# Attention values of the lead tiles: three bursts of two steps, every normalisation one step behind its sums

## The chip, the cores and the metric

One core of a Trainium2 chip. The metric is device time in microseconds (us) from launch to end. A profile of one execution tells which engine did what when: TensorE (PE, matmuls; PEld its weight loads), VectorE (DVE), ScalarE (ACT), GpSimd (POOL), and the DMA queues.

## The reference

```python
def _attn_ref(q, kv, w_sr):            # q (4, 12288, 128), kv (4, 384, 32, 128)
    kv_pool = kv.reshape(B, H // 4, 4, W // 4, 4, C).mean(axis=(2, 4))
    k = v = kv_pool.reshape(B, -1, C) @ w_sr        # 768 keys for each image
    s = (1 / sqrt(C)) * (q @ k.transpose(0, 2, 1))
    a = exp(s - s.max(-1, keepdims=True))
    a /= a.sum(-1, keepdims=True) + 1e-09
    return a @ v

def _moe_ref(x, w_gate, w_val, w_out):  # x = attention output, 49152 x 128; d_ff 1536
    return (maximum(x @ w_gate, 0) * (x @ w_val)) @ w_out
```

## The kernel before

Work goes in tiles of 512 queries, 96 of them. For one tile: six score matmuls (128 keys each) with an exponential (`scores`), the product with the values in two halves of two query blocks (`values`), the division by the sums (`keep_sums`, `keep_values`), a transposing DMA (`x_turn`), then twelve blocks of the feed-forward layer: value projection with a cast on ScalarE, gate projection with a product on VectorE, output projection. The sums of the exponentials come out of the same matmul as a 129th column, so sums and values share a PSUM bank:

```python
    def values(k, jc, half):                 # two matmuls of 128x129 into one bank
        ...
    def keep_sums(k, half):
        rinvs[k, half] = work.tile([128, 2, 1], FP32, tag="rinv", bufs=4, name="rinv")
        nc.vector.reciprocal(rinvs[k, half], x_banks[k, half][:, :, C : C + 1])

    def keep_values(k, half, engine=nc.vector):
        x_ps, rinv = x_banks.pop((k, half)), rinvs.pop((k, half))
        if engine is nc.scalar:
            for i in range(2):
                nc.scalar.mul(x16s[k][:, 2 * half + i, :], x_ps[:, i, 0:C], rinv[:, i])
        else:
            nc.vector.tensor_tensor(...)     # one product with the broadcast reciprocals

    def value_proj(k, fb):
        ...                                  # matmul, L236
        nc.scalar.copy(val, va_ps)           # the cast, L240
    def gate_proj(k, fb):
        ...                                  # matmul, L247; needs a bank
        nc.vector.scalar_tensor_tensor(      # the gate product, L250; needs the cast
            hTs[k][:, fb, :], g_ps, 0.0, vals.pop((k, fb)), op0=ALU.max, op1=ALU.mult)
```

The stages are software-pipelined: stage k does the scores of tile k, the values of tile k - 1, the projections of tile k - 3 and the output of tile k - 4. Stage k = 3 (LAG) is the first that has projections. In it the values that tiles 2 and 3 still lack are worked off from a list, two chunks of keys in each step. I call it the **lead stage**.

```python
    left = [(2, jc, 0) for jc in range(NJC - 2, NJC)]
    left += [(k, jc, half) for k, half in ((3, 0), (2, 1), (3, 1)) for jc in range(NJC)]
    ...
        for step in range(NFB):              # 12 steps in a stage
            ...                              # output projections
            if kF < NT:
                value_proj(kF, step)
            if k == LAG:
                own, left = left[:2], left[2:]
                for kV, jc, half in own:
                    values(kV, jc, half)
                    if jc == NJC - 1:
                        keep_sums(kV, half)                # VectorE
                        keep_values(kV, half, nc.scalar)   # ScalarE, at once
                        if half == 1:
                            x_turn(kV)
            ...
            if kF < NT:
                gate_proj(kF, step)
```

The softmax here doesn't subtract the row's maximum and nothing guards it: scores larger than these inputs give would overflow.

Of the kernel before, what the change touches and what calls it, by code (L numbers as in the profile page):

```python
# [16 lines left out]
def kernel(  # L17
# [22 lines left out]
    nc = tc.nc  # L40
# [5 lines left out]
    NJC = J // 128  # L46
# [20 lines left out]
    def bank(shape, dtype=FP32):  # L67
        return psum.tile(shape, dtype, tag="bank", name="bank_ps")
# [4 lines left out]
    def q_load(g):  # L73
        if not 0 <= g < NG:
            return
        b, n0 = divmod(g * GRP * T, N)
        q16 = work.tile([128, GRP * NS, C], FP16, tag="q16", bufs=2)
        nc.gpsimd.dma_start(  # L78
            q16, q[b, n0 : n0 + GRP * T, :].rearrange("(p s) c -> p s c", p=128)
        )  # L80
        q16s[g] = q16

    def q_turn(g):
        if not 0 <= g < NG:
            return
        q16 = q16s.pop(g)
        qT = work.tile([128, GRP * NS, 128], FP16, tag="qT", bufs=3)
        nc.sync.dma_start_transpose(qT, q16.rearrange("p s c -> p (s c)"))
        qTs[g] = qT
# [58 lines left out]
    def turn_open(b, pair):  # L148
        kv_Ts[b, pair] = bank([128, 2, 128])
# [33 lines left out]
    def scores(k, jc):  # L183
        if jc == 0:
            aTs[k] = work.tile([128, NJC, T], FP16, tag="aT", bufs=4, name="aT")
        s_ps = bank([128, T])
        nc.tensor.matmul(s_ps, kv16[:, k // NST, jc, 0:C], qT_of(k), start=True, stop=True)  # L187
        nc.scalar.activation(aTs[k][:, jc, :], s_ps, AF.Exp, scale=qk_scale)  # L188

    def values(k, jc, half):  # L190
        if jc == 0:
            x_banks[k, half] = bank([128, 2, C + 1])
            if half == 0:
                x16s[k] = work.tile([128, NS, C], FP16, tag="x16", bufs=3, name="x16")
        x_ps = x_banks[k, half]
        for i in range(2):
            s = 2 * half + i
            nc.tensor.matmul(  # L198
                x_ps[:, i, :], aTs[k][:, jc, s * 128 : (s + 1) * 128],
                kv16[:, k // NST, jc, C : 2 * C + 1],  # L200
                start=(jc == 0 and i == 0), stop=(jc == NJC - 1), skip_group_check=True,
# [12 lines that stand above are left out]
            nc.vector.tensor_tensor(  # L214
                x16s[k][:, 2 * half : 2 * half + 2, :], x_ps[:, :, 0:C],
                rinv.to_broadcast([128, 2, C]), op=ALU.mult,
            )

    def x_turn(k):
        x16 = x16s.pop(k)  # L220
        xT = work.tile([128, NS, 128], FP16, tag="xT", bufs=5, name="xT")
        nc.sync.dma_start_transpose(xT, x16.rearrange("p s c -> p (s c)"))
        xTs[k] = xT.rearrange("c s p -> c (s p)")
# [10 lines left out]
    def value_proj(k, fb):  # L234
        va_ps = bank([128, T])
        nc.tensor.matmul(  # L236
            va_ps, wv16[:, fb * 128 : (fb + 1) * 128], xTs[k], start=True, stop=True
        )
        val = work.tile([128, T], FP16, tag="val", bufs=6, name="val")
        nc.scalar.copy(val, va_ps)  # L240
        vals[k, fb] = val

    def gate_proj(k, fb):
        if fb == 0:
            hTs[k] = work.tile([128, NFB, T], FP16, tag="hT", bufs=3, name="hT")
        g_ps = bank([128, T])
        nc.tensor.matmul(  # L247
            g_ps, wg16[:, fb * 128 : (fb + 1) * 128], xTs[k], start=True, stop=True
        )
        nc.vector.scalar_tensor_tensor(  # L250
            hTs[k][:, fb, :], g_ps, 0.0, vals.pop((k, fb)), op0=ALU.max, op1=ALU.mult
        )
        if fb == NFB - 1:
            xTs.pop(k)
# [7 lines left out]
    def out_proj(k, fb):  # L262
        if fb == 0:
            o_banks[k] = bank([128, NS, 128])
        for s in range(NS):
            out_add(k, fb, s, o_banks[k][:, s, :], fb == 0 and s == 0)

    def out_scale(k, engine, own, o_ps=None):
        if k not in o_sbs:
            o_sbs[k] = work.tile([128, NS, 128], FP32, tag="o_sb", bufs=3, name="o_sb")  # L270
        o_sb, o_ps = o_sbs[k][:, own], o_ps if o_ps is not None else o_banks[k]
        if engine is nc.scalar:
            nc.scalar.mul(o_sb, o_ps, 1.0 / X_SCALE**2)
        else:
            nc.vector.tensor_scalar(o_sb, o_ps, 1.0 / X_SCALE**2, None, op0=ALU.mult)  # L275

    def out_store(k, own):
        nc.sync.dma_start(
            out[k // GRP * GRP * T : (k // GRP + 1) * GRP * T, :].rearrange(
                "(p i s) c -> i p s c", p=128, i=GRP  # L280
            )[k % GRP][:, own], o_sbs[k][:, own],
        )
        if own.stop == NS:
            for tiles in (hTs, o_banks, o_sbs):
                del tiles[k]
# [134 lines left out]
        keep_values(1, half)  # L420
    for jc in range(NJC - 2):
        values(2, jc, 0)
    left = [(2, jc, 0) for jc in range(NJC - 2, NJC)]
    left += [(k, jc, half) for k, half in ((3, 0), (2, 1), (3, 1)) for jc in range(NJC)]


    last = NT + LAG - 1
    for k in range(LAG, last + 1):
        g, ph = divmod(k, GRP)
        if ph == 1:  # L430
            q_turn(g + 1)
            q_load(g + 2)
        b = k // NST + 1
        at = k % NST - (NST - NJC - 6)
        for step in range(NFB):
            kO, kF = k - LAG - 1, k - LAG
            half, i = divmod(step // 2, NJC // 2)
            if k == LAG and step >= NFB - 4:
                out_proj(kF, step - NFB + 4)
            if k == LAG + 1 and step % 3 > 0:  # L440
                out_proj(kO, 4 + step - 1 - step // 3)
            if 0 <= kO:
                if kO > 0:
                    out_proj(kO, step)
                if step == NFB - 1 and k < last:
                    out_scale(kO, nc.vector if kF < NT - 2 else nc.scalar, slice(0, NS))
                    out_store(kO, slice(0, NS))
            if kF < NT:
                value_proj(kF, step)
            if k == LAG:  # L450
                own, left = left[:2], left[2:]
                for kV, jc, half in own:
                    values(kV, jc, half)
                    if jc == NJC - 1:
                        keep_sums(kV, half)
                        keep_values(kV, half, nc.scalar)
                        if half == 1:
                            x_turn(kV)
            elif step % 2 == 0:
                if k < NT:  # L460
                    scores(k, step // 2)
            elif k > GRP and k - 1 < NT:
                values(k - 1, 2 * i, half)
                values(k - 1, 2 * i + 1, half)
                if i == NJC // 2 - 1:
                    keep_sums(k - 1, half)
                    keep_values(k - 1, half)
                    if half == 1:
                        x_turn(k - 1)
            if kF < NT:  # L470
                gate_proj(kF, step)
            if k == LAG and step == 2:
                x_turn_pe(1)
            if b < B:
                if step == 1 and 0 <= at < NJC and at % 2 == 0:
                    kv_load(b, at // 2)
                if step == 3 and 0 <= at - 2 < NJC:
                    pool_pixels(nc.gpsimd, b, (at - 2) // 2, at % 2)
                pair = (at - 5) // 2
                if at % 2 == 1 and 0 <= pair < NJC // 2:  # L480
                    if step == 2:
                        turn_open(b, pair)
                        turn_add(b, pair, s3s.pop((b, pair))[:, :, None], True, True)
                    if step == 4:
                        project(b, pair)
                    if step == 8:
                        turn_values(b, pair)
# [33 lines left out]
```

## Time and profile before

| of the kernel before | value | where from |
|---|---|---|
| time | 1048.1 us (three runs, 1048.07 to 1048.92) | timed runs |
| TensorE in the chain that ended last | 97% | page |
| steady step, four matmul slots | 0.876 us | starts of the value projections |
| lead stage, k = 4, k = 5 | 8.95, 9.36, 10.67 us | order of time, starts of the value projections |
| ScalarE idle for the reciprocal (L212 for L206) | 1.5 us, three times | the waits |

The prediction shows the lines on which this rests. The first 32 us of the kernel (loads, first scores) belong to no part of the change.

### The profile page before, as it was taken

The page shows a single profiled execution, that of the slowest core. Times are in us where ns is not written, and L with a number is a line of the kernel's source. Part 1 is how long each engine was busy: PE and PEld are TensorE (multiplying, and loading weights), DVE is VectorE, ACT ScalarE, POOL GpSimd, SP SyncE. Part 2 cuts the span into 40 slices and gives each one's busy share as a digit, 9 for nine tenths or more (in the row PEclk, how much of TensorE's full clock was granted, in tenths as well). Part 3 has the DMA queues.
Part 4 walks back from the last instruction along what each step waited for, and adds up shares of the span by engine and source line. Part 5 has one row for each costly group of instructions (what it writes and reads, how often), then busy time and mean ns, then how long its engine had stood idle before and what let it go on. Part 6 is the DMA issues. An engine that isn't in the chain of part 4 may idle for free.

```text
span 1045.5 us, 25976 instructions
## 1 busy us (share of the span) xinstructions
PE 1036.0 (99%) x9984; PEld 690.1 (66%) x9984; DVE 913.3 (87%) x1679; ACT 908.9 (87%) x1741; POOL 107.8 (10%) x127
## 2 busy tenths in 40 slices
PE   8999999999999999999999999999999999999998
PEld 6566666666666666666666666666666666666665
DVE  3798889898988888998888888889988888888898
ACT  3888888888888888888888888888888888888887
POOL 2000045200000015500000003440000000000000
PEclk9999999999999999999999999999999999999999
DMA  8733256241422335623224134551331322212111
GB/s 302 120 82 74 79 177 167 52 87 32 87 53 65 72 125 138 157 57 72 58 60 87 31 87 132 150 150 41 77 65 53 72 65 54 67 32 67 32 47 47
DMA packets 125853, 90.75 MB, mean 87 GB/s; under 512 B 103328, under 2 KB 104224, under 8 KB 125728
## 3 DMA queue, kind: packets, MB, share of 16 engines
q1 hardware_dynamic: 120144, 75.78, 26.8%
q0 software_dynamic: 5440, 13.24, 7.7%
q8 instruction: 78, 1.28, 0.5%
q14 instruction: 47, 0.39, 0.1%
q10 hardware_dynamic: 144, 0.07, 0.0%
HBM read 52.76 MB, written 25.17 MB: 75 GB/s over the span
## 4 chain that ended last, share of the span: by engine, by line
PE 97%; DMA 1%; SPq 1%; DVE 0%; ACT 0%; issue 0%; DVEq 0%
PE bank_ps L257 25%; PE bank_ps L247 24%; PE bank_ps L236 24%; PE bank_ps L198 12%; PE bank_ps L187 12%; DMA parts<-in_kv_dram 1%; PE bank_ps L156 1%; PE bank_ps L168 1%; SPq L128 0%; ACT aT L188 0%; SPq L93 0%; PE bank_ps L176 0%; DVE kv L169 0%; DVE kvT L163 0%; PE bank_ps L229 0%
## 5 line engine op out<-in xcount | busy, mean ns | idle before, releaser
L250 DVE SCALAR_TENSOR_TENSOR hT<-bank_ps,val 128x512 f16<-128x512 f32 x1152 | 759.5, 687 | 100.9 <-ACT val L240 74.7
L240 ACT CAST val<-bank_ps 128x512 f16<-128x512 f32 x1152 | 677.7, 591 | 111.8 <-PE bank_ps L236 107.5
L257 PEld LDWEIGHTS <-hT 128*128 128x128 f16 x4608 | 351.4, 98 | 200.1 <-issue 0.9
L257 PE MATMUL bank_ps<-wo,hT 128*128 128x128 f16 x4608 | 443.1, 219 | 0.0
L236 PE MATMUL bank_ps<-xT,wv 128*128 128x512 f16 x1152 | 436.6, 379 | 0.0
L247 PE MATMUL bank_ps<-xT,wg 128*128 128x512 f16 x1152 | 435.7, 378 | 0.0
L188 ACT ACTIVATE aT<-bank_ps 128x512 f16<-128x512 f32 x576 | 346.0, 604 | 16.9 <-PE bank_ps L187 16.6
L198 PE MATMUL bank_ps<-kv,aT 128*128 128x129 f16 x2304 | 223.3, 219 | 0.0
L198 PEld LDWEIGHTS <-aT 128*128 128x128 f16 x2304 | 177.2, 98 | 68.1 <-issue 0.6
L187 PE MATMUL bank_ps<-qT,kv 128*128 128x512 f16 x576 | 216.4, 379 | 1.1 <-DVE kv L169 0.5
L247 PEld LDWEIGHTS <-wg 128*128 128x128 f16 x1152 | 111.5, 97 | 65.8 <-issue 0.5
L236 PEld LDWEIGHTS <-wv 128*128 128x128 f16 x1152 | 112.7, 98 | 0.5
L214 DVE TENSOR_TENSOR x<-bank_ps,rinv 128x256 f16<-128x256 f32 x188 | 79.7, 424 | 6.7 <-DVE rinv L206 0.2
L78 POOL DMA_DIRECT2D q<-in_q_dram x23 | 12.5, 545 | 570.6 <-DMA qT<-q 570.4
L275 DVE TENSOR_SCALAR o_sb<-bank_ps 128x512 f32<-128x512 f32 (+1 forms) x95 | 64.0, 674 | 1.3 <-PE bank_ps L257 1.3
L139 POOL TENSOR_TENSOR s<-parts 128x512 f32<-128x512 f32 x36 | 45.3, 1269 | 162.7 <-DMA parts<-in_kv_dram 153.5
L187 PEld LDWEIGHTS <-kv 128*128 128x128 f16 x576 | 55.8, 98 | 2.4 <-DVE kv L169 1.4
L206 DVE RECIPROCAL rinv<-bank_ps 128x2 f32<-128x2 f32 x192 | 30.6, 160 | 1.6 <-PE bank_ps L198 1.6
L141 POOL TENSOR_TENSOR s<-s 128x512 f32<-128x512 f32 x18 | 22.9, 1269 | 1.4
L143 POOL TENSOR_TENSOR c<-s 128x256 f32<-128x256 f32 x18 | 13.1, 726 | 1.4
L163 DVE COPY kvT<-bank_ps 128x256 f32<-128x256 f32 x12 | 5.0, 417 | 4.5 <-PE bank_ps L156 4.5
L146 POOL TENSOR_TENSOR kv_s<-c 128x128 f32<-128x128 f32 x18 | 8.2, 456 | 1.4
(37 smaller groups left out, 81.0 us busy)
## 6 DMA issues: line engine op xcount, KB each, us to landing
parts<-in_kv_dram SPq DMA_DIRECT2D x48, 512.0 KB, 6.4
out_dram<-o_sb SPq DMA_DIRECT2D x95, 256.0 KB, 2.1
q<-in_q_dram POOLq DMA_DIRECT2D x23, 512.0 KB, 5.1
xT<-x SPq DMA_TRANSPOSE x94, 2.5
q<-in_q_dram SPq DMA_DIRECT2D x1, 768.0 KB, 8.3
wv<-in_moe_w_val_dram POOLq DMA_DIRECT2D x2, 192.0 KB, 4.3
wg<-in_moe_w_gate_dram POOLq DMA_DIRECT2D x2, 192.0 KB, 4.9
wo<-in_moe_w_out_dram POOLq DMA_DIRECT2D x1, 384.0 KB, 9.3
```

The source lines that it names most:

```text
L139: eng.tensor_tensor(s2[:, i], parts[:, 2 * i, h], parts[:, 2 * i + 1, h], op=ALU.add)
L187: nc.tensor.matmul(s_ps, kv16[:, k // NST, jc, 0:C], qT_of(k), start=True, stop=True)
L188: nc.scalar.activation(aTs[k][:, jc, :], s_ps, AF.Exp, scale=qk_scale)
L198: nc.tensor.matmul(x_ps[:, i, :], aTs[k][:, jc, s * 128 : (s + 1) * 128], kv16[:, k // NST, jc, C : 2 * C + 1], start=(jc == 0 and i == 0) ...
L206: nc.vector.reciprocal(rinvs[k, half], x_banks[k, half][:, :, C : C + 1])
L214: nc.vector.tensor_tensor(x16s[k][:, 2 * half : 2 * half + 2, :], x_ps[:, :, 0:C], rinv.to_broadcast([128, 2, C]), op=ALU.mult,)
L236: nc.tensor.matmul(va_ps, wv16[:, fb * 128 : (fb + 1) * 128], xTs[k], start=True, stop=True)
L240: nc.scalar.copy(val, va_ps)
L247: nc.tensor.matmul(g_ps, wg16[:, fb * 128 : (fb + 1) * 128], xTs[k], start=True, stop=True)
L250: nc.vector.scalar_tensor_tensor(hTs[k][:, fb, :], g_ps, 0.0, vals.pop((k, fb)), op0=ALU.max, op1=ALU.mult)
L257: nc.tensor.matmul(o_ps, hTs[k][:, fb, s * 128 : (s + 1) * 128], wo16[:, fb, :], start=first, stop=(fb == NFB - 1), skip_group_check=True,)
L275: nc.vector.tensor_scalar(o_sb, o_ps, 1.0 / X_SCALE**2, None, op0=ALU.mult)
```

## The change

Its intent: the normalisation on ScalarE shall not stand at the head of the queue before its reciprocal is there. It is issued a step later, behind the next cast. And the value matmuls, evenly two chunks a step, are gathered into bursts: three chunks in each of two steps, then a step with none, in which the two scalings lie. (The first pair of scalings is the exception: step 0 keeps its two chunks, and the scalings of its sums lie in step 1, the first step of a burst.)

```diff
-    left = [(2, jc, 0) for jc in range(NJC - 2, NJC)]
-    left += [(k, jc, half) for k, half in ((3, 0), (2, 1), (3, 1)) for jc in range(NJC)]
+    left = {0: (2, 0, range(NJC - 2, NJC))}
+    for step, k, half in ((1, 3, 0), (4, 2, 1), (7, 3, 1)):
+        left[step] = (k, half, range(NJC // 2))
+        left[step + 1] = (k, half, range(NJC // 2, NJC))
+    ready = {}
@@ in the step loop
             if k == LAG:
-                own, left = left[:2], left[2:]
-                for kV, jc, half in own:
-                    values(kV, jc, half)
-                    if jc == NJC - 1:
-                        keep_sums(kV, half)
-                        keep_values(kV, half, nc.scalar)
-                        if half == 1:
-                            x_turn(kV)
+                if step in ready:
+                    keep_values(*ready[step], nc.scalar)
+                    if ready[step][1] == 1:
+                        x_turn(ready[step][0])
+                if step in left:
+                    kV, hV, own = left[step]
+                    for jc in own:
+                        values(kV, jc, hV)
+                    if own.stop == NJC:
+                        keep_sums(kV, hV)
+                        ready[step + 1] = (kV, hV)
```

## The prediction

> **What bounds the kernel now.** I read the page's busy row first. TensorE (PE) is at 99%, but that row says little: a 128x512 matmul is listed with 379 ns, while the order of time shows the next one starting 0.22 us later. So I went to the chain of work that ended last, to see which engine holds the end.
>
> ```profile
> PE 1036.0 (99%) x9984; PEld 690.1 (66%) x9984; DVE 913.3 (87%) x1679; ACT 908.9 (87%) x1741; POOL 107.8 (10%) x127
> ...
> PE 97%; DMA 1%; SPq 1%; DVE 0%; ACT 0%; issue 0%; DVEq 0%
> ```
>
> TensorE holds 97% of the end. A change that moves work among other engines can win only where TensorE waits. The diff touches one stage, the lead stage (k = LAG = 3), the first that runs the feed-forward projections, so I put the timeline of one engine at a time over it. Its twelve steps begin with the value projections (L236) at 31.91 us and end at 40.86, where the next stage (k = 4) begins; k = 5 begins at 50.22 and k = 6 at 60.89.
>
> How much does TensorE lose there? Count slots. A slot is one 512-column matmul or four 128-column ones. A steady step has four (value projection, scores or attention values, gate projection, output projection). Between 900.22 and 942.29 the value projection starts 48 times, so a step is 42.07 / 48 = 0.876 us and a slot 0.219 us. The lead stage has 24 projections, 10 slots of attention values (20 steps of two matmuls, from the list `left`), 4 of output projection and 1 turn: 39 slots, 8.54 us; it took 8.95, a loss of 0.41. Stage k = 4 has 24 + 6 scores + 8 output slots = 38, 8.32 us; it took 9.36, a loss of 1.04. Stage k = 5 has 48, 10.51 us; it took 10.67, a loss of 0.16. Afterwards the steps are regular. **The most that any repair of the lead stage can give is 0.41 + 1.04 + 0.16 = 1.6 us, 0.15% of the time.**
>
> Why does TensorE lose it? The scalar engine's own order of time:
>
> ```profile
> 32.82 0.63 ACT L212 ACTIVATE x<-bank_ps,rinv 128x128 f16<-128x128 f32 x2
> 33.34 1.77 ACT L240 CAST val<-bank_ps 128x512 f16<-128x512 f32 x3
> 35.69 0.63 ACT L212 ACTIVATE x<-bank_ps,rinv 128x128 f16<-128x128 f32 x2 [0.57 <-DVE rinv L206]
> 36.20 1.56 ACT L240 CAST val<-bank_ps 128x512 f16<-128x512 f32 x3
> 38.22 0.63 ACT L212 ACTIVATE x<-bank_ps,rinv 128x128 f16<-128x128 f32 x2 [0.46 <-DVE rinv L206]
> 38.74 1.56 ACT L240 CAST val<-bank_ps 128x512 f16<-128x512 f32 x3
> 40.76 0.63 ACT L212 ACTIVATE x<-bank_ps,rinv 128x128 f16<-128x128 f32 x2 [0.46 <-DVE rinv L206]
> 41.27 1.56 ACT L240 CAST val<-bank_ps 128x512 f16<-128x512 f32 x3
> 42.69 0.64 ACT L188 ACTIVATE aT<-bank_ps 128x512 f16<-128x512 f32 x1
> ```
>
> At three of the four normalisations (L212) the scalar engine stands for 0.57 + 0.46 + 0.46 = 1.49 us until the reciprocal of the sums (L206) is there. The vector engine shows why that is late:
>
> ```profile
> 36.82 1.29 DVE L250 SCALAR_TENSOR_TENSOR hT<-bank_ps,val 128x512 f16<-128x512 f32 x2 [0.58 <-ACT val L240]
> 38.02 0.16 DVE L206 RECIPROCAL rinv<-bank_ps 128x2 f32<-128x2 f32 x1
> 38.10 0.67 DVE L250 SCALAR_TENSOR_TENSOR hT<-bank_ps,val 128x512 f16<-128x512 f32 x1
> ```
>
> The reciprocal stands behind the gate product (L250) of the step before, which needed a cast (L240) that ended only just before. Meanwhile the scalar engine, its queue headed by the normalisation, makes no further cast, and VectorE then idles 0.58 us for one. The two take turns: 35.69, 38.22, 40.76 is one round per three steps in 2.53 us, while TensorE's nine slots take 1.97. So TensorE runs into banks that were not emptied, and the chain in order of time says so twice:
>
> ```profile
> 38.49 0.37 ACT x L212
> 38.86 0.04 issue
> 38.90 0.38 PE bank_ps L236
> ...
> 41.04 0.35 ACT x L212
> 41.39 0.04 issue
> 41.43 0.38 PE bank_ps L187
> ```
>
> Both times the matmul wants the bank that the normalisation reads.
>
> **What the Trainium skill says.** "Trainium Kernel Development and Optimization", Performance Expectations, warns that matmul busy time is a bad metric because matmuls are pipelined; the trace agrees (379 ns listed, 0.22 us apart). "TensorE: Matmul & The Clock Gate", Part 1, gives start to start as N / 2.4 GHz plus some 2.5 ns, 216 ns for 512 columns; the trace has 0.22. "PSUM — Partial Sum Buffer", Engine vs sequencer instructions, calls the ScalarE and VectorE queues strict FIFO: the idle pieces above are that, a cast that is ready stands behind a normalisation that is not. "ScalarE: Activation LUTs", What ACT_TABLE_LOAD costs, has an ACTIVATE with a pointer operand at 280 ns + 0.833 ns an element, 387 ns for 128, with some 93 ns of overlap; the trace lists 364 ns, and a pair until the next cast takes 41.27 - 40.76 = 0.51 us.
>
> **The change, part by part.** *Removed and added work: none.* The same 40 value matmuls, four reciprocals, eight scalings and two transposing DMAs run; only positions change.
>
> *One step behind.* The queue of ScalarE now has cast, cast, scalings instead of cast, scalings, cast. The cast of the next step (0.47 us back to back: 41.27 to 42.69 is three) fills the time in which the gate product and the reciprocal run. The wait of 0.46 is removed by 0.47 of cast, the one of 0.57 all but 0.1. Saved on ScalarE: about 1.4 of 1.49 us.
>
> *Bursts.* In place of one slot of values in each of steps 0 to 9, there is one in step 0 and 1.5 in steps 1, 2, 4, 5, 7, 8, none in 3, 6, 9. Three steps still have nine slots (1.97 us); inside them the value projections are 0.77, 0.77 and 0.44 us apart instead of 0.66. The light step is the one that holds the two scalings. ScalarE needs 3 x 0.47 + 0.51 = 1.92 us for three steps, VectorE 3 x 0.61 + 0.08 = 1.91 (0.61 is half of the 1.29 of two products without their end; 0.08 from 38.02 to 38.10): all three engines come out nearly level. A cast may now wait for a matmul in a burst. Laying the casts out step by step (0.42 us from a projection's start to its cast, as 31.91 to 32.33) I find such waits of about 0.3 near the turn in step 2 and 0.45 near step 9, where output projection begins.
>
> *Sum at the start of k = 4.* Before, the cast of its first step began at 41.27 + 2 x 0.47 = 42.2; its matmul had begun at 40.86, so it was 42.2 - 41.28 = 0.9 late. After, TensorE without loss arrives at 31.91 + 8.54 = 40.45, so the cast could begin at 40.87; ScalarE gets there at 32.33 + 12 x 0.47 + 4 x 0.51 = 40.0 plus the waits of 0.8 or so and a few small ones, 40.9 to 41.1: 0.2 late at most. The two bank waits go, since each normalisation comes 1 us earlier against the same taker.
>
> *Stage k = 4.* Here ScalarE is the slower engine: its round of an exponential and two casts takes 1.43 us for two steps (42.69, 44.12, 45.56 are the exponentials), 8.58 for the stage, TensorE 8.32. Lateness grows from 0.2 to about 0.5. At 50.34, where the old kernel had recovered to 0.5 late, TensorE lost nearly nothing more; so I charge 0 to 0.3 us, plus about 0.1 for the uneven start. From k = 5 on TensorE is slower (1.75 us for two steps) and the lateness dissolves. Gain: 1.6 - 0.3 = **1.3 us**, or 1048.1 - 1.3 = **1046.8 us**.
>
> **Rivals.** (1) *The bursts starve ScalarE:* the wait for the reciprocal becomes a wait for projections. For it: the engines are level within 3%, with no slack in a round. Against: the wait sits where ScalarE would otherwise be ahead. It would halve the gain, 1047.5. (2) *VectorE becomes the bound:* its lead stage is 12 x 0.61 + 0.5 for reciprocals and the turn, near 8 us of TensorE's 8.54; it idled 0.58 a round only because of ScalarE. Gain 0.8 to 1, 1047.2. (3) *A late normalisation delays the transposing DMA, hence k = 5 and 6:* the old one was issued at 38.87 and was done in 4.05 us, k = 5 begins at 50.22, 7 us later. I expect nothing. (4) *Nothing arrives at the end:* no wait for memory stands after the stage in the chain, so what TensorE gains early it keeps.
>
> **Range and chances.** The ceiling is 1.6 us; three runs of the kernel before lie 0.85 us apart, as large as the gain. I take 1046.0 (whole ceiling and a good draw) to 1048.3 (no gain). Two per cent is 21 us, thirteen times the ceiling, so within 2% is nearly certain.
>
> **What would show it.** Right: no idle of 0.4 us or more for L206 before L212; no piece of L212 in the chain that ended last; k = 4 starting some 0.4 us and k = 5 about 1.2 to 1.5 us earlier; steady steps at 0.876 us as before. Wrong: ScalarE's idle reappearing before L240 with the value projection as releaser, or a projection held by a bank that a normalisation still owns. A shift outside 30 to 61 us would mean that something I have not seen moved.

## The result, and the profile after

| | before | after | ratio, 95% interval |
|---|---|---|---|
| first comparison, 6 runs each | 1048.43 us | 1046.67 us | 0.9988, 0.9974 to 1.0002 |
| second, 9 and 5 runs | 1047.91 us | 1046.66 us | 0.9984, 0.9972 to 0.9997 |
| third, 9 and 5 runs | 1047.82 us | 1046.58 us | 0.9991, 0.9979 to 1.0004 |

Times are medians. A ratio is the mean time of the one kernel's runs over that of the other's in the same rounds, so it is not quite the ratio of the medians. The timed runs alone barely resolve the gain: one interval of three leaves 1 out. Both kernels have the odd run at a granted clock of 0.996 or 0.997 (after: 1048.92 and 1049.16; before: 1049.67 and 1049.97), longer than the change is worth. One such execution was traced (vector_norm_timed, 0.998): all that it has more lies before the lead stage, which begins at 34.16 us against 32.57 in the other trace of that kernel. So the runs below are judged by a finer measure: **the stretch** from the first value projection of the lead stage to the first of stage k = 6, read from the order of time. All that the change can do lies in it, and it repeats: 28.98 and 28.99 us in two traces of the kernel before, 27.83, 27.83 and 27.82 in three of the kernel after. What comes behind the stretch (the span less the end of the stretch) lasts 984.6 us to within 0.1 in every trace of every run, so what is won in the stretch arrives at the end.

| us | lead stage | k = 4 | k = 5 | stretch |
|---|---|---|---|---|
| before | 8.95 | 9.36 | 10.67 | 28.98 |
| after | 8.57 | 8.63 | 10.63 | 27.83 |
| slots of 0.219 us | 39: 8.54 | 39: 8.54 | 48: 10.51 | 126: 27.6 |

The stretch is 1.15 us shorter, which agrees with medians 1.2 to 1.8 us apart. Here is ScalarE's order of time after, in the columns start, length, instruction, and idle time before it with its releaser:

```profile
32.91 1.24 ACT L240 CAST val<-bank_ps 128x512 f16<-128x512 f32 x2 [0.25 <-PE bank_ps L236]
34.05 0.63 ACT L212 ACTIVATE x<-bank_ps,rinv 128x128 f16<-128x128 f32 x2
34.56 0.59 ACT L240 CAST val<-bank_ps 128x512 f16<-128x512 f32 x1
35.34 0.58 ACT L240 CAST val<-bank_ps 128x512 f16<-128x512 f32 x1 [0.18 <-PE bank_ps L236]
35.82 0.63 ACT L212 ACTIVATE x<-bank_ps,rinv 128x128 f16<-128x128 f32 x2
36.33 1.63 ACT L240 CAST val<-bank_ps 128x512 f16<-128x512 f32 x3
37.85 0.63 ACT L212 ACTIVATE x<-bank_ps,rinv 128x128 f16<-128x128 f32 x2
38.36 1.08 ACT L240 CAST val<-bank_ps 128x512 f16<-128x512 f32 x2
39.73 0.59 ACT L240 CAST val<-bank_ps 128x512 f16<-128x512 f32 x1 [0.29 <-PE bank_ps L236]
40.21 0.63 ACT L212 ACTIVATE x<-bank_ps,rinv 128x128 f16<-128x128 f32 x2
40.73 1.57 ACT L240 CAST val<-bank_ps 128x512 f16<-128x512 f32 x3
42.14 0.65 ACT L188 ACTIVATE aT<-bank_ps 128x512 f16<-128x512 f32 x1
```

No normalisation (L212) has idle time before it. What idle time is left names the value projection (L236) as releaser: ScalarE waits for TensorE now, as it should where TensorE is the bound. VectorE, in the same stretch, stands less: before, it stood 0.58 us for a cast three times, each one product after a reciprocal; now only 0.22 us behind the reciprocal at 34.80 and 0.23 at 41.35. Around the middle one it has no idle time:

```profile
36.13 1.52 DVE L250 SCALAR_TENSOR_TENSOR hT<-bank_ps,val 128x512 f16<-128x512 f32 x2
37.56 0.16 DVE L206 RECIPROCAL rinv<-bank_ps 128x2 f32<-128x2 f32 x1
37.64 2.04 DVE L250 SCALAR_TENSOR_TENSOR hT<-bank_ps,val 128x512 f16<-128x512 f32 x3
```

And in the chain that ended last, at the place where the score matmul (L187) of k = 4 waited for a normalisation, there is now only TensorE, a slot at a time:

```profile
41.00 0.22 PE bank_ps L247
41.22 0.22 PE bank_ps L236
41.44 0.22 PE bank_ps L187
```

The span of the first trace after, 1044.9 us, is only 0.6 below the 1045.5 of before, less than the stretch gives. The rest went in the head: the lead stage began at 32.49 us against 31.91. I do not put that down to the change, which edits no instruction there. The start strays from trace to trace of one kernel (32.08 to 32.49 in three traces after; 31.79 and 31.91 in two before; 32.57 and 34.16 in two of vector_norm below, which has no bursts; 31.83 in vector_burst, which has them), and in the chain of the head it is the first loads that land later: their piece in the chain lasted 11.22 us in place of 10.82.

### The profile page after: what moved, and what is told of

Same layout as the page of the kernel before. It is cut to its first block, busy times and chain, and to the rows that moved or that the text cites. A ratio compares the mean times of both kernels' runs of the same rounds, so it can differ in the third digit from the quotient of the medians.

```text
span 1044.9 us, 25975 instructions
## 1 busy us (share of the span) xinstructions
PE 1034.5 (99%) x9984; PEld 689.0 (66%) x9984; DVE 913.4 (87%) x1679; ACT 908.5 (87%) x1741; POOL 107.6 (10%) x127
## 4 chain that ended last, share of the span: by engine, by line
PE 97%; DMA 1%; SPq 1%; DVE 0%; issue 0%; ACT 0%; DVEq 0%
PE bank_ps L257 25%; PE bank_ps L236 24%; PE bank_ps L247 24%; PE bank_ps L198 12%; PE bank_ps L187 12%; DMA parts<-in_kv_dram 1%; PE bank_ps L156 1%; PE bank_ps L168 1%; SPq L128 0%; ACT aT L188 0%; SPq L93 0%; PE bank_ps L176 0%; DVE kv L169 0%; DVE kvT L163 0%; PE bank_ps L229 0%
## 5 line engine op out<-in xcount | busy, mean ns | idle before, releaser
L257 PEld LDWEIGHTS <-hT 128*128 128x128 f16 x4608 | 351.1, 97 | 199.8 <-issue 0.2
L257 PE MATMUL bank_ps<-wo,hT 128*128 128x128 f16 x4608 | 443.6, 219 | 0.0
L236 PE MATMUL bank_ps<-xT,wv 128*128 128x512 f16 x1152 | 437.1, 379 | 0.0
L188 ACT ACTIVATE aT<-bank_ps 128x512 f16<-128x512 f32 x576 | 346.6, 605 | 17.5 <-PE bank_ps L187 17.2
L187 PE MATMUL bank_ps<-qT,kv 128*128 128x512 f16 x576 | 216.6, 379 | 1.0 <-DVE kv L169 0.5
L236 PEld LDWEIGHTS <-wv 128*128 128x128 f16 x1152 | 112.5, 98 | 0.7
L187 PEld LDWEIGHTS <-kv 128*128 128x128 f16 x576 | 55.7, 98 | 2.4 <-DVE kv L169 1.4
```

The costliest lines, as they stand in the source:

```text
L187: nc.tensor.matmul(s_ps, kv16[:, k // NST, jc, 0:C], qT_of(k), start=True, stop=True)
L188: nc.scalar.activation(aTs[k][:, jc, :], s_ps, AF.Exp, scale=qk_scale)
L236: nc.tensor.matmul(va_ps, wv16[:, fb * 128 : (fb + 1) * 128], xTs[k], start=True, stop=True)
L257: nc.tensor.matmul(o_ps, hTs[k][:, fb, s * 128 : (s + 1) * 128], wo16[:, fb, :], start=first, stop=(fb == NFB - 1), skip_group_check=True,)
```

## The experiments

**Theory A:** the wait of the normalisation, at the head of a queue that works strictly in order, for a reciprocal behind the gate product is what cost the time; moving the normalisation behind the next cast fills it. **Theory B:** the bursts do it, since they give a light step for the scalings. **Rival C:** it is the 2.0 us of scalings on ScalarE itself, wherever it waits. First, how far a trace repeats, and the change once more. (const_norm, late_sums, two_behind and the first vector_norm ran on another chip, where the kernel before took 1047.62 us, once.)

**before_again and after_again**, no edit.

> The kernel before, profiled once more, to learn how well a trace repeats. Measure used for all runs: the stretch from the first value projection of the lead stage to the first one of stage k = 6; 28.98 us in the first trace of the kernel before, 27.83 after, 27.6 if TensorE lost nothing (126 slots of 0.219 us). Every theory: 28.98 within 0.1 us again, with three idle pieces of about 0.5 us on ScalarE before a normalisation. If it strays by 0.4 us or more, the stretch can't be used to tell anything.

> The changed kernel, timed in five rounds and profiled again. Every theory: stretch 27.83 within 0.1 us; time 1.2 us (0.11%) below the kernel before, ratio near 0.9988, with an interval that may still hold 1.

Measured: 28.99 and 27.83 us, each within 0.01 of its first trace; the time of after_again as in the table. The stretch can be used to a few hundredths.

**behind_only**: one step behind, but spread evenly.

```diff
+                if step in ready:
+                    keep_values(*ready[step], nc.scalar)
+                    if ready[step][1] == 1:
+                        x_turn(ready[step][0])
                 own, left = left[:2], left[2:]
                 for kV, jc, half in own:
                     values(kV, jc, half)
                     if jc == NJC - 1:
                         keep_sums(kV, half)
-                        keep_values(kV, half, nc.scalar)
-                        if half == 1:
-                            x_turn(kV)
+                        ready[step + 1] = (kV, half)
```

> Half of the change: values spread evenly as before (two chunks a step), but each normalisation one step behind its sums. Theory A (the place of the normalisation in ScalarE's queue is what counts): stretch 27.7 to 28.0, no idle before a normalisation for the reciprocal, time like the changed kernel's. Theory B (the bursts are needed, because they give the light step in which the scalings fit): stretch 28.3 or more.

Measured: stretch 27.98 us, no idle before L212; 1047.37 us, ratio 0.999 (0.9977 to 1.0002). Theory A holds: 1.00 of the 1.15 us comes from the place in the queue alone.

```profile
35.80 0.63 ACT L212 ACTIVATE x<-bank_ps,rinv 128x128 f16<-128x128 f32 x2
...
37.74 0.67 ACT L212 ACTIVATE x<-bank_ps,rinv 128x128 f16<-128x128 f32 x2
...
40.35 0.63 ACT L212 ACTIVATE x<-bank_ps,rinv 128x128 f16<-128x128 f32 x2
```

The median of its time is 0.7 us above after_again's, more than the 0.15 of the stretch. The start of the lead stage strays by as much (31.77 to 32.57 us in all traces but the one at 34.16).

**burst_only**: the bursts, each normalised in the step of its sums.

```diff
                     if own.stop == NJC:
                         keep_sums(kV, hV)
-                        ready[step + 1] = (kV, hV)
+                        keep_values(kV, hV, nc.scalar)
+                        if hV == 1:
+                            x_turn(kV)
```

and without the `if step in ready` part.

> The other half: bursts as in the change, each normalisation in the step of its sums as before. Theory A: the reciprocal still stands behind the gate product of the step before, idle of 0.3 us or more at three normalisations, stretch 28.6 to 29.0. Theory B: a burst step is 0.77 us long, so the gate product of the step before is done in time; idle under 0.2 us each, stretch 28.2 or less.

Measured: stretch 28.54 us, 0.44 below before, between the two expectations; 1047.4 us, ratio 0.9991 (0.9976 to 1.0006). The idle time is as theory A said:

```profile
35.19 0.63 ACT L212 ACTIVATE x<-bank_ps,rinv 128x128 f16<-128x128 f32 x2 [0.35 <-DVE rinv L206]
...
37.73 0.63 ACT L212 ACTIVATE x<-bank_ps,rinv 128x128 f16<-128x128 f32 x2 [0.46 <-DVE rinv L206]
...
40.27 0.63 ACT L212 ACTIVATE x<-bank_ps,rinv 128x128 f16<-128x128 f32 x2 [0.46 <-DVE rinv L206]
```

Theory B's reason fails: the bursts did not make the reciprocal ready in time. Where do the 0.44 us come from? One of the three pieces is 0.22 us shorter (0.35 for 0.57). And before, the run of three casts after the first normalisation took 1.77 us, since ScalarE also stood there for the turn of step 2; here no run of three takes more than 1.56, which is 0.21 less. The sum is 0.43. A burst ends a tile's sums one step earlier (steps 2, 5, 8 in place of 3, 6, 9), which moves the normalisation to another place against the turn; that this is the reason is argued, not tried by itself. The two halves do not add up: 1.00 and 0.44 us alone, 1.15 together.

**const_norm**: the normalisation in its old place, multiplying by a constant, so that it need not wait. Wrong result on purpose (the diff is shortened).

```diff
+    one = const.tile([128, 2, 1], FP32)
+    nc.vector.memset(one, 1.0)
@@ lead stage
-                        keep_values(kV, half, nc.scalar)
+                        keep_values(kV, half, nc.scalar, one)   # scales by one, not by rinv
```

> Wrong result on purpose: the kernel before, the normalisations of the lead stage in their old place, but scaling by a constant 1.0 from a tile filled at the start; the reciprocals still run, nobody waits for them. Theory A (the wait for the reciprocal is the cost): idle on ScalarE for the reciprocal gone, stretch 27.7 to 28.1. Rival (the 2.0 us of scalings on ScalarE are the cost wherever they wait): stretch 28.6 or more.

Measured: stretch 28.97 us, as before to 0.01. Not because theory A is wrong: the wait is still there, though the reciprocal's result is not read.

```profile
35.61 0.63 ACT L213 ACTIVATE x<-bank_ps,one 128x128 f16<-128x128 f32 x2 [0.57 <-DVE rinv L206]
...
38.14 0.62 ACT L213 ACTIVATE x<-bank_ps,one 128x128 f16<-128x128 f32 x2 [0.46 <-DVE rinv L206]
...
40.67 0.62 ACT L213 ACTIVATE x<-bank_ps,one 128x128 f16<-128x128 f32 x2 [0.46 <-DVE rinv L206]
```

The operands are the bank and `one`, the releaser is the reciprocal. Sums and values share a bank, and the compiled program lets only one engine at a time at it. The Trainium skill, "PSUM — Partial Sum Buffer", PSUM bank collisions raise a hardware error, says why: reads of one bank by ScalarE and VectorE at once collide as well as writes do. No run here shows a collision; the wait that avoids it shows.

**sums_elsewhere**: so the reciprocal has to leave the bank too. It reads the constant tile, at the same place on VectorE (shortened). Its output is wrong, which doesn't matter for the time.

```diff
-                        keep_sums(kV, half)
-                        keep_values(kV, half, nc.scalar)
+                        keep_sums(kV, half, one)                # reciprocal of one, not of the bank
+                        keep_values(kV, half, nc.scalar, one)
```

> Wrong result on purpose, the sharper form of const_norm, whose normalisation still waited for the reciprocal (the same three idle pieces, 0.57, 0.46, 0.46 us) although it did not read its result: both read the same bank, and the compiled program orders them. Here the reciprocal of the lead stage reads a constant tile instead of the bank, at the same place on VectorE, so neither data nor bank ties the normalisation to it. Theory A (the wait is the cost): the idle before the normalisations falls under 0.2 us each, stretch 27.7 to 28.2. Rival (the scalings in the old place cost the time by themselves): stretch 28.6 or more.

Measured: stretch 27.65 us, 0.05 over the slots of TensorE and just under the range of theory A; 1046.09 us, once.

```profile
34.87 0.63 ACT L215 ACTIVATE x<-bank_ps,one 128x128 f16<-128x128 f32 x2
35.38 1.57 ACT L243 CAST val<-bank_ps 128x512 f16<-128x512 f32 x3
36.84 0.64 ACT L215 ACTIVATE x<-bank_ps,one 128x128 f16<-128x128 f32 x2
```

The same scalings stand in the same place of the queue, the bursts are absent, and the loss is gone. Rival C falls, and theory A is shown from the side of its cause: take the wait away, and the time goes. (No run cut the tie of the bank while it kept the tie of the data, so how the wait divides between the two stays open.)

**late_sums**: the wait made longer. Reciprocal and normalisation follow the gate product of their own step, so one more product stands before them (shortened).

```diff
-                    if jc == NJC - 1:
-                        keep_sums(kV, half)
-                        keep_values(kV, half, nc.scalar)
-                        ...
             if kF < NT:
                 gate_proj(kF, step)
+            if k == LAG and done:            # the sums completed in this step
+                keep_sums(kV, half)
+                keep_values(kV, half, nc.scalar)
+                ...
```

> The suspected wait doubled: the kernel before with each reciprocal (and its normalisation) put after the gate product of the same step, so that it stands behind one more product of 0.61 us. Theory A: each of the waits grows from 0.5 to about 1.1 us at four places, stretch 28.98 + 4 x 0.6 = 31.4, 30.6 or more. Rival (ScalarE's idle is mostly hidden under TensorE's own time): stretch under 29.6.

Measured: stretch 31.93 us, 2.95 longer than before; 1050.43 us, once.

```profile
33.75 0.62 ACT L212 ACTIVATE x<-bank_ps,rinv 128x128 f16<-128x128 f32 x2 [0.90 <-DVE rinv L206]
...
37.27 0.62 ACT L212 ACTIVATE x<-bank_ps,rinv 128x128 f16<-128x128 f32 x2 [1.45 <-DVE rinv L206]
...
40.46 0.62 ACT L212 ACTIVATE x<-bank_ps,rinv 128x128 f16<-128x128 f32 x2 [1.12 <-PE bank_ps L257]
...
43.65 0.62 ACT L212 ACTIVATE x<-bank_ps,rinv 128x128 f16<-128x128 f32 x2 [1.12 <-DVE rinv L206]
```

The idle pieces sum to 0.90 + 1.45 + 1.12 + 1.12 = 4.59 us against 1.49, so 3.1 us of idle bought 2.95 us of stretch. (The third piece names a matmul; the reciprocal stands at the same place there, and a wait for several signals is put down to the last that the profile saw.)

**two_behind**: the changed kernel with two steps in place of one.

```diff
-                        ready[step + 1] = (kV, hV)
+                        ready[step + 2] = (kV, hV)
```

> The changed kernel with each normalisation two steps behind its sums in place of one. Theory A: one step covers the reciprocal already; nothing more to gain, stretch 27.75 to 28.0. Rival (what is left, 0.24 us over the floor, is still the reciprocal): stretch 27.65 or less. A third way: the bank of the sums is held a step longer, a projection waits for it, stretch 28.2 or more with a normalisation in the chain.

Measured: stretch 27.99 us; 1047.09 us, once. One step is enough; a second costs 0.16, with no normalisation in the chain. The last normalisation stands in step 10 here and in behind_only, in step 9 in the changed kernel, and the two that have it in step 10 agree, 27.99 and 27.98. So the 0.15 us that the bursts add to behind_only go with ending the sums a step earlier.

**vector_norm** (and again with rounds, vector_norm_timed): the normalisation in its old place, on VectorE.

```diff
-                        keep_values(kV, half, nc.scalar)
+                        keep_values(kV, half)
```

> The kernel before with the four normalisations of the lead stage on VectorE (as in all later stages): 2.0 us off ScalarE, 4 x 0.34 us onto VectorE, no hand-over. Theory A with VectorE as the next bound: its lead stage becomes 8.0 + 1.4 = 9.4 us against TensorE's 8.54, it catches up 0.4 us in k = 4, stretch 28.2 to 28.7. If it is 27.9 or less, VectorE had more room than I counted; at 29 or more the place of the work does not matter.

> The kernel before with the lead normalisations on VectorE, timed: stretch 27.71 again within 0.1, time at the changed kernel's or 0.1 us below it, ratio to before near 0.9987.

Measured: stretch 27.71 us in both traces, under the range that I had set. The first ran once, in 1046.8 us. Timed, 1047.56 us, ratio 0.9995 (0.9982 to 1.0009), 1 us above what I expected: two of its five runs had a clock of 0.996 and 0.998 (1048.82, 1048.41), and the best was 1046.29. VectorE does take a round of three steps in longer than TensorE's 1.97 us:

```profile
35.95 0.16 DVE L206 RECIPROCAL rinv<-bank_ps 128x2 f32<-128x2 f32 x1
...
38.27 0.16 DVE L206 RECIPROCAL rinv<-bank_ps 128x2 f32<-128x2 f32 x1
...
40.60 0.16 DVE L206 RECIPROCAL rinv<-bank_ps 128x2 f32<-128x2 f32 x1
40.80 0.42 DVE L214 TENSOR_TENSOR x<-bank_ps,rinv 128x256 f16<-128x256 f32 x1
41.14 4.87 DVE L250 SCALAR_TENSOR_TENSOR hT<-bank_ps,val 128x512 f16<-128x512 f32 x8
46.16 1.29 DVE L250 SCALAR_TENSOR_TENSOR hT<-bank_ps,val 128x512 f16<-128x512 f32 x2 [0.16 <-ACT val L240]
```

A round is 2.32 us, so it falls behind by some 0.35 us in a round: counted from 0.42 us after the start of their gate matmul, its products begin 0.38, 0.84 and 1.20 us late in steps 0, 3 and 6. In step 9 it is 1.10, for from step 8 on output projections lengthen TensorE's round. Yet TensorE's lead stage took 8.57 us, no more than in the changed kernel. VectorE works off what has piled up from 41.14 without a gap and waits for a cast again at 46.16. Being late cost nothing here. I take it that free banks took up the lag, which no run tried by itself. The error of my expectation is plain either way: I charged the excess of busy time to the end. It also fits a rule of the skill ("ScalarE: Activation LUTs", Rules for kernel authors: multiplications belong on VectorE): one product of 424 ns takes the place of two scalings of 364 ns, and the hand-over falls away. (The reason that the page gives, speed in bf16, is not tested here.)

**vector_burst** and **after_third**: bursts with the normalisation on VectorE at once, beside the changed kernel.

```diff
                     if own.stop == NJC:
                         keep_sums(kV, hV)
-                        ready[step + 1] = (kV, hV)
+                        keep_values(kV, hV)
+                        if hV == 1:
+                            x_turn(kV)
```

> The bursts of the change with the normalisations on VectorE at once. If bursts help by giving a light step, stretch 27.60 to 27.70, at the floor of 27.6; if they only mattered to ScalarE, 27.71 as without them.

> The changed kernel beside the two above on one chip: stretch 27.83 within 0.1 us; time within 0.3 us of vector_norm, not to be told apart by the clock.

Measured: stretches 27.71 and 27.82 us; times 1046.29 us (ratio 0.9988, 0.9976 to 1.0001) and 1046.58 us (0.9991). Without scalings on ScalarE the bursts change nothing (27.71 with and without). By the trace vector_burst and vector_norm beat the changed kernel by 0.12 us; the timed runs cannot tell them apart: it is a hundredth of a per cent.

**All runs in one line of thought.** ScalarE gets to its first exponential (L188) of stage k = 4 after all casts and normalisations of the lead stage. Put its start, counted from the first value projection, beside the stretch:

| us | first exponential of k = 4 | against before | stretch | against before |
|---|---|---|---|---|
| before | 10.78 | | 28.98 | |
| const_norm | 10.77 | -0.01 | 28.97 | -0.01 |
| burst_only | 10.33 | -0.45 | 28.54 | -0.44 |
| two_behind | 9.83 | -0.95 | 27.99 | -0.99 |
| behind_only | 9.82 | -0.96 | 27.98 | -1.00 |
| after | 9.65 | -1.13 | 27.83 | -1.15 |
| vector_norm | 9.51 | -1.27 | 27.71 | -1.27 |
| vector_burst | 9.51 | -1.27 | 27.71 | -1.27 |
| sums_elsewhere | 9.51 | -1.27 | 27.65 | -1.33 |
| late_sums | 13.73 | +2.95 | 31.93 | +2.95 |

A microsecond of lateness on ScalarE goes with a microsecond at the end, over a range of four microseconds, although TensorE is the bound of the kernel. The table alone shows only that the two go together; that ScalarE's wait drives both is shown by late_sums and sums_elsewhere, which changed the wait. In k = 4 ScalarE needs 1.43 us for two steps and TensorE as much (39 slots in six pairs of steps, 1.42), so what ScalarE brings along from the lead stage it can't make up there. Before, its cast was 0.93 us late at the start of k = 4 and 0.17 at the start of k = 5; after, 0.19 and 0.14 (late: beyond 0.42 us after the start of its projection). Before, the lateness went because TensorE was held up, not because ScalarE caught up: it had no idle time in k = 4.

## Why the prediction was right

The time, 1046.67 us for 1046.8, and the mechanism hold. That the two are 0.13 us apart is partly luck: the prediction starts from 1048.1 us, the kernel before had a median of 1048.43 in the comparison, and the start of the lead stage alone strays by 0.4 us between traces of the kernel after. The stretch is the fairer test. By its steps:

- **The ceiling of 1.6 us was mis-sized.** I gave stage k = 4 38 slots. From one first value projection to the next there are 39: the output projection of tile 1 in step 0 of k = 5 is issued ahead of that step's value projection (the order of time has nine groups of L257 between 40.86 and 50.22 us, not eight). So stage k = 4 lost 0.82 and not 1.04 us, and the ceiling is 1.4 us (28.98 - 27.6).
- **What is left, 0.1 to 0.4 us by the text and taken as 0.3, was slightly too much:** it is 27.83 - 27.6 = 0.23. The two errors, 0.2 and 0.07 us, cancel in part, and 1.3 us predicted stand against 1.15 in the stretch.
- **Waits on ScalarE:** all of the 1.49 us went. The new waits for a projection came where I had laid them, smaller: 0.18 us near the turn for 0.3, and 0.29 near step 9 for 0.45.
- **Lateness at the start of k = 4, "0.2 late at most":** the first exponential begins at 42.14, so the cast ahead of it (0.47 back to back) at 41.67; its matmul at 41.06 plus 0.42 is 41.48. It was 0.2 late, and 0.9 before. It grew to 0.47 in the last step of k = 4, for the 0.5 said. The reason given, ScalarE slower over the stage (8.58 us for 8.32), counted one slot too few: TensorE's 39 take 8.54. The 39th stands at the very end of the stage, and there the lateness falls again, to 0.14 at the start of k = 5.
- **The bank waits** went as said: the third normalisation came 5.36 us after the first projection for 6.31, the fourth 7.72 for 8.85, "1 us earlier".
- **Signs named ahead:** counted from the start of the lead stage, k = 4 begins 0.38 us earlier (0.4 said), k = 5 1.11 (1.2 to 1.5 said, a little short), steady steps unchanged. The one shift outside the stretch is the later head (above); with it, k = 4 began 0.2 us later by the trace's own clock (41.06 for 40.86).
- **Rival 1** took part at a small size (0.18 + 0.29 us of new waits, without effect on the lead stage, 8.57 us for 39 slots of 8.54). **Rival 2** did not occur, and vector_norm shows that VectorE had room even for the normalisations. **Rivals 3 and 4:** nothing of them; what follows the stretch lasts 984.6 us before and after.
- **Missed:** that the wait was one for the bank too, not only for the reciprocal's value (const_norm). It did not change the number here, as the change moves both.

## What to carry to other kernels

In an engine that works in order, put behind a hand-over the instruction that is ready meanwhile, not the one that needs its answer; one step of distance was enough, and two were slightly worse. Do not judge an engine by whether it is the bound of the kernel on the average: find the stage in which its lag cannot be made up, and there every microsecond of its idle time counts, while a lag of the same size on an engine that can catch up before its neighbours run dry cost nothing. And when a trace names a releaser, check whether the tie is data or a shared bank before an experiment cuts one of them.

## What the Trainium skill lacked or had wrong

- "PSUM — Partial Sum Buffer", PSUM bank collisions raise a hardware error: it says that readers of one bank must be kept apart, not what this costs in time. Here a ScalarE instruction waited 0.57, 0.46 and 0.46 us for a VectorE read of another column of its bank (const_norm, 28.97 us); without that read the stretch was 27.65 us. Whether two banks for such columns would pay was not tried here.
- "ScalarE: Activation LUTs", What ACT_TABLE_LOAD costs: the estimates from its formulas are near but somewhat long. A cast of 512 columns is 613 ns by the page and 591 ns here; a scaling of 128 with a pointer operand 387 ns by the page and 364 ns here (613 and 387 ns are estimates worked out from the page's formulas, and so is the prediction's 387). Back to back the overlap was some 0.12 us (591 ns long, 0.47 us apart), where the page has 93 ns.
- No page that I read says how to tell an engine's harmless lag from a costly one. Here VectorE fell behind by up to 1.20 us with no loss on TensorE in the lead stage (vector_norm, 8.57 us), and ScalarE's lateness at the start of k = 4 came back one for one.
